# Half chunk's transposes in two PSUM tiles and earlier, outputs scaled by halves, one load behind one transpose

## The chip, the cores and the metric

The kernel runs on one core of one Trainium2 chip. The metric is the device time of one launch in microseconds (us), lower is better. The kernel before took 320.49 us, the median of three runs (318.17, 320.49 and 322.54).

## The reference

Eight batches of 576 rows go through a retention layer (attention with a decay and no softmax) with 8 heads of 64, and its output x, 512 wide, goes through a mixer of rank 32 and a two-layer MLP:

```python
scores = scale * np.matmul(q, k.transpose(0, 1, 3, 2))
Dmat = np.where(rel >= 0, gamma[:, None, None] ** rel[None, :, :], 0.0)
ret = scores * Dmat[None, :, :, :]
attn = np.matmul(ret, v)                        # x: heads side by side
h = xt @ U @ V                                  # U: 576 x 32, V: 32 x 576
u = x + h.transpose(0, 2, 1)
ch = np.maximum(u @ w_ch1, 0.0) @ w_ch2         # 512 -> 2048 -> 512
return (u + ch).astype(np.float32)
```

Inputs and output are float32; the kernel computes in bfloat16 with float32 accumulation.

## The kernel before, in words

Two batches make a pair of 1152 rows, cut into nine chunks of 128 rows (`NI = 9`). Chunk 4 (`J`) is shared: its lower 64 partitions (`LO`) hold the last rows of the even batch, its upper 64 (`HI`) the first rows of the odd one. These are the half chunks.

**The decay** is split into a factor per key row (`vscale`, put into v) and one per query row (`qscale`, put into the output), so that a running 64 by 64 state per head carries all earlier rows. A chunk needs: casts of q and k to bf16; transposes of both; scores from the transposed ones (`SC`); a causal mask (`mask`); keys times values into the state (`ST`); state copies to bf16 (`Sblk`); masked scores times values (`RV`) and queries times state (`QS`), both into one PSUM tile `po`; and the scaling of `po` by `qscale` into x (`XS`).

**Pair 0** is done in a written order. Its rows outside chunk 4 are four units of 256 rows, 0 to 3, two chunks each; functions that end in `_u` treat a unit, those in `_J` a half chunk. TensorE transposes q and k there (`T_u` at L656, `T_J` at L805). `startup` runs units 0 and 1 and `LO` (batch 0) up to u transposed (`uT`); short runs of matmuls on the identity (`warm`, L213) fill places in between. `first_stretch` goes on with the first MLP layer of batch 0 (`Y1`, L550), and between its blocks `HI` and units 2 and 3 (batch 1). In `T_J` the eight transposes, keys first, go to one PSUM tile `pst`; ScalarE copies the keys out (L757), VectorE the queries in two copies (L759). The two read one PSUM bank, and VectorE's copies wait for ScalarE's. The unit tile `po` has two banks, one for each 128 rows; `XS_u` (L737) scales both in one instruction.

Towards the end of `startup`, in order on TensorE: state products of unit 1's lower half (`ST_u`, L748), one `warm`, values of unit 1 (`RV_u`, L720), `T_J(LO)` (L811), the upper half's state products, scores of `LO` (`SC_J`, L830), `QS_u` of unit 1 (L729), transposes of x (`to_xT`, L979), `RV_J` and `QS_J` (L856, L866), the mixer's U product (`MA`, L454), the V product (L1000), and `Y1`. On VectorE: the copies of the queries, the mask of `LO` (L844), `XS_u(1)`, `XS_J(LO)` (L873).

**The later stretches**, b = 1 to 7, are lists: the MLP of batch b (in stretch 1 also the second layer of batch 0) is the main list, in a fixed order on TensorE. `merge` puts other items in where the finished share of the main list's cost reaches their place, a number from 0 to 1: `fills` (sections S, casts C, masks M, value swaps W of the next batch's chunks, and the mixer), and `places`, for each stretch the loads and the preps. `load` (L254) issues three or six DMAs on SP's queue; `prep` casts q on ScalarE (L270), k on VectorE or GpSimd (L268), scales v on GpSimd (L279) and issues a transposing DMA (`xbar`, L287) on SP. SP issues in program order: a step whose input is late holds all behind it. The mixer's `MT` also transposes u by DMA from SP (L508).

In stretch 1 the chunks of batches 2 and 3 (pair 1) are handled. Its preps are those of chunks 2 to 8 of pair 1, its loads those of chunks 4 to 8 of pair 1 and chunk 0 of pair 2:

```python
1: ((0.11, 0.24, 0.41, 0.53, 0.70, 0.85),
    (0.06, 0.20, 0.32, 0.47, 0.60, 0.73, 0.90)),
```

So the load of chunk 8 (0.70) is on SP ahead of chunk 7's transposing DMA (0.73). The section at 0.92 scores chunks 6 and 7.

The first-layer weights are one SBUF tile `w1_sb`, filled by four DMAs of 512 columns on GpSimd's queue (L219).

Of the kernel before, what the change touches and what calls it, by code (L numbers as in the profile page):

```python
# [36 lines left out]
def kernel(  # L37
# [17 lines left out]
    P = 128  # L55
# [63 lines left out]
    w1_sb = consts.tile([P, NCC, dff], BF16, name="w1_sb")  # L119
# [96 lines left out]
    W1B = 512  # L216

    def load_w1(fb):
        nc.gpsimd.dma_start(  # L219
            out=w1_sb[:, :, fb * W1B:(fb + 1) * W1B],  # L220
            in_=moe_w_ch1[:, fb * W1B:(fb + 1) * W1B].rearrange("(c p) f -> p c f", p=P),
        )
# [312 lines left out]
    def y1_items(par, by_seg=False):  # L535
# [6 lines left out]
        def Y1(f, seg):  # L542
# [6 lines left out]
            for cc in range(NCC):  # L549
                nc.tensor.matmul(  # L550
                    ps[:, 0:n, :], w1_sb[:, cc, f * P:(f + 1) * P],
                    st["uT", par][:, c0:c0 + n, cc, :],
                    start=(cc == 0), stop=(cc == NCC - 1),
                )
# [67 lines left out]
    def load_u(u, which):  # L622
        b = u // 2
        t0 = 2 * P * (u % 2) + HALF * b
        for j in which:
            dram = (q, k, v)[j]
            for hh in range(2):
                t = stage.tile([P, H, D], FP32, tag="stage", name="stage_t")
                un[u]["f", j, hh] = t
                nc.sync.dma_start(  # L630
                    out=t.rearrange("p (h j) d -> p h (j d)", j=2),
                    in_=dram[b, 4 * hh:4 * hh + 4, t0:t0 + 2 * P, :].rearrange(
                        "h (p j) d -> p h (j d)", j=2),
                )

# [23 lines left out]
    def T_u(u, j, eng):  # L659
        pst = ps_big.tile([P, 2 * NHP, P], BF16, tag="big", name="pst")  # L660
        for jj in range(2):
            for hp in range(NHP):
                nc.tensor.transpose(
                    pst[:, jj * NHP + hp, :], un[u][j][:, jj, hp * P:(hp + 1) * P], ident)
        t = qkT_pool.tile([P, 2 * NHP, P], BF16, tag="qkT", name="qkT")
# [7 lines left out]
        if eng is nc.scalar:  # L673
            nc.scalar.activation(out=o, in_=i_, func=AF.Copy)
        else:
            eng.tensor_copy(out=o, in_=i_)
# [214 lines left out]
    def pss_tile():  # L891
        return ps_s.tile([P, NHP, P], FP32, tag="pss", name="pss")

    def cast_unit(u):
        for j in (1, 0):
            for hh in range(2):
                cast_u(u, j, hh, nc.gpsimd)

    def startup():
        load_u(0, (1, 0))  # L900
        load_v_rows()
        load_u(1, (1, 0))
        load_u(0, (2,))
        load_u(1, (2,))
        load_J(LO, (1, 0, 2))
        load_u_rows()
        load_J(HI, (1, 0, 2))
        load_u(2, (1, 0, 2))
        load_u(3, (1, 0, 2))
        nc.gpsimd.memset(x_of(0, J)[HI, :], 0.0)  # L910

        warm(10)
        cast_unit(0)
        T_u(0, 1, nc.vector)
        late_consts()
        warm(5)
        nc.scalar.activation(out=V_b, in_=V_f, func=AF.Copy)
        T_u(0, 0, nc.scalar)
# [4 lines left out]
        cast_unit(1)  # L923
        T_u(1, 1, nc.scalar)
# [3 lines left out]
        T_u(1, 0, nc.scalar)  # L928
        scale_u(0, 0, nc.gpsimd)
        load_w1(0)  # L930
        scale_u(1, 0, nc.gpsimd)
        scale_u(1, 1, nc.gpsimd)
        cast_J(LO, nc.gpsimd, (0,))
        scale_J(LO, nc.gpsimd)
        load_w1(1)
        cast_J(HI, nc.gpsimd, (1, 0))
        scale_J(HI, nc.gpsimd)
        load_w1(2)
        scale_u(0, 1, nc.vector)
# [5 lines left out]

        accA = pss_tile()
        accB = ps_big.tile([P, NHP, P], FP32, tag="big", name="pss2")
        ST_u(0, LO, accA, True)
        Sblk(accA, 0)
        ST_u(0, ALL, accB, True)  # L950
        Sblk(accB, 1)
        cast_J(LO, nc.scalar, (1,))
# [19 lines left out]
        XS_u(1)  # L972
        make_ue()

        xT = [ps_big.tile([P, dm], FP32, tag="big", name="xT") for _ in range(3)]

        def to_xT(i, ccs):
            for cc in ccs:
                nc.tensor.matmul(  # L979
                    xT[cc][:, i * P:(i + 1) * P],  # L980
                    x_of(0, i)[:, cc * P:(cc + 1) * P], ident,
                    start=(i == 0), stop=True, skip_group_check=True,
                )

        for i in range(2):
            to_xT(i, range(3))
# [3 lines left out]
        MA_, _, _, _ = mixer_items(0, 0, split=True)  # L990
        MA_(steps=(0, J))
        xT.append(ps_o.tile([P, dm], FP32, tag="po", name="xT"))
        to_xT(2, range(3))
        MA_(steps=(J, J + 1))
        to_xT(3, range(3))
        for i in range(J):
            to_xT(i, (3,))
        for cc in range(NCC):
            g = slice(cc * R, (cc + 1) * R)
            nc.tensor.matmul(  # L1000
                xT[cc], st["a", 0][g, :], V4[g, HALF:HALF + 4 * P],
                start=False, stop=True, skip_group_check=True,
            )
        warm(1)
        for cc in range(NCC):
            o = st["uT", 0][:, :, cc, :]
            i_ = xT[cc].rearrange("p (s t) -> p s t", t=P)
            if cc % 2 == 0:
                nc.scalar.activation(out=o, in_=i_, func=AF.Copy)  # L1009
            else:  # L1010
                nc.vector.tensor_copy(out=o, in_=i_)

    def gated_w2(f, block):

        nc.gpsimd.tensor_copy(
            out=gate[0:1, 0:1], in_=st["y1", 1][0:1, block, P:P + 1])
        load_w2(f)

    def first_stretch():

        ys = iter([fn for _, fn in y1_items(0)])

        def y(n):
            for _ in range(n):
                fn = next(ys, None)
                if fn is not None:
                    fn()

        _, MH0, _, outs0 = mixer_items(0, 0, split=True)
        MA1, MH1, MT1, outs1 = mixer_items(0, 1, split=True)  # L1030
        y(1)
        make_uo()
        y(3)
        T_J(HI, (nc.scalar, nc.vector), ps_s, "pss")
        y(1)
        SC_J(HI)
        mask_J(HI)
        acc = pss_tile()
        ST_J(HI, acc, 0)
        Sblk(acc, 0, hps=slice(0, 2))  # L1040
        y(1)
        RV_J(HI)
        XS_J(HI)
        ST_J(HI, acc, 1)
        Sblk(acc, 0, hps=slice(2, 4))

        def unit(u, slots, last):
            for hh in range(2):
                cast_u(u, 1, hh, nc.gpsimd)
            cast_u(u, 0, 0, nc.gpsimd)  # L1050
            cast_u(u, 0, 1, nc.gpsimd)
            if last:
                load(*order[NI], (1, 0, 2), gate=True)
                load(*order[NI + 1], (1, 0, 2))
            scale_u(u, 0, nc.gpsimd)
            if not last:
                load_w1(u + 1)
            scale_u(u, 1, nc.gpsimd)
            if not last:
                y(1)  # L1060
            T_u(u, 1, nc.vector)
            T_u(u, 0, nc.scalar)
            y(2)
            SC_u(u, 0, ps_sc, "psc")
            mask_u(u, 0)
            y(1)
            ST_u(u, LO, acc, False)
            Sblk(acc, slots[1], (nc.scalar, nc.scalar) if last else (nc.vector, nc.scalar))
            SC_u(u, 1, ps_sc, "psc")
            mask_u(u, 1)  # L1070
            if not last:
                RV_u(u, 0)
                ST_u(u, HI, acc, False)
                Sblk(acc, slots[2])
            else:
                y(1)
                load(*order[NI + 2], (1, 0, 2))
                RV_u(u, 0)
            QS_u(u, 0, slots[0])
            QS_u(u, 1, slots[1])  # L1080
            RV_u(u, 1)
            XS_u(u)

        unit(2, (0, 1, 2), False)
        unit(3, (2, 3), True)
# [3 lines left out]
        xT = [None] * NCC  # L1089

# [150 lines left out]
```

## Time and profile before

| | |
|---|---|
| median of three runs | 320.49 us |
| the profiled execution's own time | 318.2 us |
| its span, first to last instruction | 316.4 us |
| TensorE (PE) busy | 306.7 us, 97% |
| VectorE (DVE) busy | 168.0 us, 53% |
| ScalarE (ACT) busy | 138.3 us, 44% |
| GpSimd (POOL) busy | 90.5 us, 29% |
| granted TensorE clock | 1.000 |

Times in the profile are from the span's start. PE is matmuls, PEld their weight loads, SPq the queue of SyncE. A row of the timeline reads: start, length, engine, line, operation, output and inputs, shapes, count, and in brackets how long the engine had been idle before and who ended that. Matmul ends are modelled, so a short wait can lie inside a row of PE. The chain of work that ended last lists start, length and instruction of each step, each released by the one above. A line can be that of a helper: L757 and L759 are `copy`, which several steps use.

### The profile page before, as it was taken

How to read it: one execution, taken by the hardware profiler on the slowest of the kernel's cores; microseconds unless marked ns; L12 is line 12 of the kernel's file. 1: busy time of each engine (PE TensorE's matmuls, PEld its weight loads, DVE VectorE, ACT ScalarE, POOL GpSimd, SP SyncE). 2: the span in 40 equal slices, each digit the busy share in tenths (PEclk: the TensorE clock that was granted, in tenths of full speed). 3: DMA queues.
4: the chain of work that ended last, by engine and by line, in shares of the span. 5: the costliest groups of instructions: out<-in, count | busy, mean ns of one | idle time of the engine just before them, and what ended most of it. 6: DMA issues, size and time to landing. Idle time of an engine off the chain costs nothing.

```text
span 316.4 us, 9192 instructions
## 1 busy us (share of the span) xinstructions
PE 306.7 (97%) x3940; PEld 168.9 (53%) x3966; DVE 168.0 (53%) x331; ACT 138.3 (44%) x285; POOL 90.5 (29%) x139
## 2 busy tenths in 40 slices
PE   8989999999999999999999999999999999999995
PEld 3564654654544454467654445467645444467544
DVE  6872656436997853993258724892368614100012
ACT  3756657760231575147820474147720463057300
POOL 6862834512322422253301430352301100200000
PEclk9999999999999999999999999999999999999999
DMA  7999999999999999999929696999634105110022
GB/s 214 274 200 285 206 206 217 199 186 244 202 204 256 250 217 155 256 238 224 185 70 209 191 214 137 216 238 233 152 64 138 68 2 85 66 67 2 0 98 70
DMA packets 149881, 53.31 MB, mean 168 GB/s; under 512 B 129008, under 2 KB 147312, under 8 KB 149840
## 3 DMA queue, kind: packets, MB, share of 16 engines
q1 hardware_dynamic: 143072, 40.40, 62.7%
q0 software_dynamic: 6768, 12.32, 16.2%
q8 instruction: 31, 0.51, 0.7%
q14 instruction: 10, 0.08, 0.1%
HBM read 36.85 MB, written 9.44 MB: 146 GB/s over the span
## 4 chain that ended last, share of the span: by engine, by line
PE 81%; DVE 7%; DMA 4%; SPq 3%; issue 2%; ACT 2%; POOL 1%; DVEq 0%; ACTq 0%; POOLq 0%
PE ps_y L550 39%; PE ps_y L584 29%; DMA qkT<-qk 2%; SPq L254 2%; DMA stage_t<-in_q_dram 2%; DVE ret L348 1%; DVE o_sb L573 1%; PE ps_y L595 1%; PE po L398 1%; DVE s_f L370 1%; PE psc L318 1%; PE ph L490 1%; DVE xt L737 1%; PE pa L454 1%; PE po L409 1%
## 5 line engine op out<-in xcount | busy, mean ns | idle before, releaser
L550 PE MATMUL ps_y<-uT,w_sb 128*128 128x512 bf16 (+3 forms) x768 | 130.3, 326 | 0.5 <-ACT uT L1009 0.4
L584 PE MATMUL ps_y<-w_sb,y 128*128 128x512 bf16 x534 | 122.6, 379 | 2.8 <-issue 1.9
L555 ACT ACTIVATE y<-ps_y 128x384 bf16<-128x384 f32 (+2 forms) x192 | 89.3, 490 | 49.8 <-PE ps_y L550 48.9
L550 PEld LDWEIGHTS <-w_sb 128*128 128x128 bf16 x768 | 71.1, 98 | 51.7 <-issue 2.1
L584 PEld LDWEIGHTS <-y 128*128 128x128 bf16 x560 | 52.7, 98 | 61.2
L573 DVE TENSOR_TENSOR o_sb<-ps_y,u 128x512 f32<-128x512 f32 (+2 forms) x38 | 25.1, 661 | 55.6 <-PE ps_y L584 53.3
L377 ACT ACTIVATE s_sb<-s_f 128x1024 bf16<-128x1024 f32 (+1 forms) x16 | 14.8, 922 | 82.1 <-DVE s_f L370 75.6
L576 POOL DMA_DIRECT2D out_dram<-o_sb x31 | 17.4, 562 | 112.7 <-DVE o_sb L573 103.1
L417 DVE TENSOR_TENSOR xt<-po,qscale 128x512 bf16<-128x512 f32 x27 | 17.6, 686 | 43.8 <-PE po L409 43.8
L279 POOL TENSOR_TENSOR vt<-stage_t,vscale 128x512 bf16<-128x512 f32 x27 | 28.1, 1042 | 41.0 <-DMA stage_t<-in_v_dram 39.0
L348 DVE TENSOR_TENSOR ret<-psc,tri 64x512 bf16<-64x512 f32 (+1 forms) x64 | 38.6, 603 | 1.2
L496 DVE TENSOR_TENSOR u<-ph,xt 128x512 bf16<-128x512 f32 (+4 forms) x33 | 22.5, 734 | 13.1 <-PE ph L490 13.0
L270 ACT ACTIVATE qk<-stage_t 128x512 bf16<-128x512 f32 x27 | 16.8, 623 | 12.0 <-DMA stage_t<-in_q_dram 11.9
L268 POOL CAST qk<-stage_t 128x512 bf16<-128x512 f32 x20 | 12.3, 617 | 18.7 <-DMA stage_t<-in_k_dram 12.7
L370 DVE TENSOR_TENSOR s_f<-inc,s_f 128x256 f32<-128x256 f32 x38 | 16.1, 423 | 2.1 <-PE inc L335 0.5
L361 DVE COPY vs<-vt 64x256 bf16<-64x256 bf16 x54 | 14.7, 271 | 1.0
L699 DVE TENSOR_TENSOR ret<-psc,triU 128x1024 bf16<-128x1024 f32 x8 | 9.6, 1220 | 5.2 <-PE psc L691 5.2
L648 POOL CAST qk<-stage_t 128x512 bf16<-128x512 f32 x16 | 9.7, 616 | 8.5 <-DMA stage_t<-in_q_dram 5.5
L213 PE MATMUL pw<-ident 128*128 128x512 bf16 x31 | 10.3, 462 | 1.4 <-POOL ident masks.py:199 1.4
L398 PEld LDWEIGHTS <-qkT 64*64 64x64 bf16 x384 | 4.7, 108 | 6.4 <-issue 5.9
L318 PE MATMUL psc<-qkT 64*64 64x64 bf16 x432 | 7.3, 196 | 0.4 <-DMA qkT<-qk 0.4
L652 POOL TENSOR_TENSOR qk<-stage_t,vscaleU 128x512 bf16<-128x512 f32 x7 | 7.3, 1059 | 1.0 <-DMA stage_t<-in_v_dram 1.0
(122 smaller groups left out, 179.1 us busy)
## 6 DMA issues: line engine op xcount, KB each, us to landing
stage_t<-in_k_dram SPq DMA_DIRECT2D x32, 256.0 KB, 4.2
stage_t<-in_q_dram SPq DMA_DIRECT2D x32, 256.0 KB, 4.7
stage_t<-in_v_dram SPq DMA_DIRECT2D x32, 256.0 KB, 5.4
out_dram<-o_sb POOLq DMA_DIRECT2D x31, 256.0 KB, 3.8
w_sb<-in_moe_w_ch_dram POOLq DMA_DIRECT2D x4, 512.0 KB, 7.6
w_sb<-in_moe_w_ch_dram POOLq DMA_DIRECT2D x8, 256.0 KB, 5.8
out_dram<-o_sb SPq DMA_DIRECT2D x4, 256.0 KB, 2.0
stage_t<-in_k_dram SPq DMA_DIRECT2D x6, 128.0 KB, 4.8
```

The lines of the kernel that those rows point to most:

```text
L270: nc.scalar.activation(out=t[rows, 0, :], in_=c["f", 0][rows].rearrange("p h d -> p (h d)"), func=AF.Copy)
L279: (eng or nc.gpsimd).tensor_tensor(out=c["v"][rows], in0=c["f", 2][rows], in1=vscale[rows, i, :, None].to_broadcast([n, H, D]), op=ALU.mult,)
L348: nc.vector.tensor_tensor(out=ret[o, n, 0:m], in0=psc[t, hl, 0:m * D].rearrange("p (b i) -> p b i", i=D), in1=tri[t, None, t].to_broadcast ...
L370: nc.vector.tensor_tensor(out=s_f[:, s, :], in0=src, in1=s_f[:, st["f_end"], :], op=ALU.add)
L377: nc.scalar.activation(out=s_sb[:, 0:n, :], in_=s_f[:, 0:n, :], func=AF.Copy)
L417: nc.vector.tensor_tensor(out=x_of(pr, i).rearrange("p (hp hl d) -> p hl hp d", hl=2, d=D), in0=po[:, :, a * SW:(a + 1) * SW].rearrange("p ...
L496: nc.vector.tensor_tensor(out=st["u", par][:, i0 - base:i0 - base + n, w].rearrange("p s (c d) -> p c s d", c=len(ccs)), in0=t[:, :, 0:n, ...
L550: nc.tensor.matmul(ps[:, 0:n, :], w1_sb[:, cc, f * P:(f + 1) * P], st["uT", par][:, c0:c0 + n, cc, :], start=(cc == 0), stop=(cc == NCC - 1),)
L555: nc.scalar.activation(out=st["y1", par][:, f, c0 * P:(c0 + n) * P], in_=ps[:, 0:n, :].rearrange("p s t -> p (s t)"), func=AF.Relu)
L573: nc.vector.tensor_tensor(out=o_sb[:, 0:n], in0=ps[:, 0:n], in1=st["u", par][:, c, w], op=ALU.add)
L576: (nc.sync if last else nc.gpsimd).dma_start(out=out_flat[r0:r0 + P, w], in_=o_sb[:, 0:n])
L584: nc.tensor.matmul(ps, st["y1", par][:, f, c * P:(c + 1) * P], w2_sb[:, f, :], start=(f == 0), stop=(f == NF - 1),)
```

## The change

`startup`, `first_stretch` and their helpers become one flat function `front`. Engine by engine, its instructions are the same in the same order, but for these:

1. `T_J` takes a PSUM tile for the keys and one for the queries. For `LO` both come from `ps_big`, for `HI` one from `ps_s` and one from `ps_o`.
2. `T_J(LO)` stands ahead of `RV_u(1, ...)` on TensorE, in the place of one `warm`; `QS_u(1, ...)` stands ahead of the upper half's `ST_u` and of `SC_J(LO)`.
3. `XS_u(1)` and `XS_u(3)` are two instructions each, 128 rows apiece; the mask of `LO` is between unit 1's two. Of unit 3, chunk 7's transposes are now written ahead of chunk 8's for two columns of x.
4. In stretch 1 the loads at 0.70 and 0.85 go to 0.76 and 0.88, the prep at 0.90 to 0.93. On SP this swaps one pair: chunk 7's transposing DMA comes ahead of chunk 8's three loads. No other order changes, on any engine.
5. `w1_sb` is four tiles of 512 columns; loads, matmuls and waits on it are the same.

```diff
-    w1_sb = consts.tile([P, NCC, dff], BF16, name="w1_sb")
+    w1_t = [consts.tile([P, NCC, W1B], BF16, name=f"w1_{n}") for n in range(dff // W1B)]
...
-    def T_J(r, engs, pool_=None, tag="big"):
+    def T_J(r, engs, k_at=None, q_at=None):
         c = ch[0, J]
-        pst = (pool_ or ps_big).tile([P, 2 * NHP, P], BF16, tag=tag, name="pst")
-        for j in (1, 0):
+        pst = {}
+        for j, (pool_, tag) in ((1, k_at or (ps_big, "big")), (0, q_at or (ps_big, "big"))):
+            pst[j] = pool_.tile([P, NHP, P], BF16, tag=tag, name="pst")
             for x in range(2):
                 for t in range(2):
                     nc.tensor.transpose(
-                        pst[:, j * NHP + 2 * x + t, r], c["qk"][r, j, (2 * t + x) * P:(2 * t + x + 1) * P],
+                        pst[j][:, 2 * x + t, r], c["qk"][r, j, (2 * t + x) * P:(2 * t + x + 1) * P],
                         ident[r, r])
...
-        copy(engs[0], c["kT"][:, :, r], pst[:, NHP:, r])
+        copy(engs[0], c["kT"][:, :, r], pst[1][:, :, r])
         o = c["qkT"][:, 0:NHP, r].rearrange("p (g x) (n t) -> p x t g n", g=2, t=2)
-        i_ = pst[:, 0:NHP, r].rearrange("p (x t) (g n) -> p x t g n", t=2, g=2)
+        i_ = pst[0][:, :, r].rearrange("p (x t) (g n) -> p x t g n", t=2, g=2)
         for x in range(2):
             copy(engs[1], o[:, x], i_[:, x])
...
         warm(1, ps_big, "big")
-        ST_u(1, LO, accB, False)
-        Sblk(accB, 2)
-        warm(1, ps_big, "big")
+        ST_u(1, LO, acc[1], False)
+        Sblk(acc[1], 2)
+        T_J(LO, (ACT, DVE))
         RV_u(1, 0)
         RV_u(1, 1)
-        T_J(LO, (nc.scalar, nc.vector))
-        ST_u(1, HI, accB, False)
-        Sblk(accB, 3)
-        SC_J(LO)
-        mask_J(LO)
         QS_u(1, 0, 1)
         QS_u(1, 1, 2)
-        XS_u(1)
+        ST_u(1, HI, acc[1], False)
+        Sblk(acc[1], 3)
+        SC_J(LO)
+        XS_u(1, 0, 1)
+        mask_J(LO)
+        XS_u(1, 1, 2)
         make_ue()
...
-        T_J(HI, (nc.scalar, nc.vector), ps_s, "pss")
+        T_J(HI, (ACT, DVE), (ps_s, "pss"), (ps_o, "po"))
...
-            XS_u(u)
+        XS_u(3, 0, 1)
+        XS_u(3, 1, 2)
...
-            1: ((0.11, 0.24, 0.41, 0.53, 0.70, 0.85),
-                (0.06, 0.20, 0.32, 0.47, 0.60, 0.73, 0.90)),
+            1: ((0.11, 0.24, 0.41, 0.53, 0.76, 0.88),
+                (0.06, 0.20, 0.32, 0.47, 0.60, 0.73, 0.93)),
```

More of the change, by code (lines that the diff above doesn't have):

```diff
@@ L672, in T_u @@
             i_ = pst.rearrange("p (j hp) t -> p j hp t", j=2)
[L673 to L676, printed above, removed]
+        copy(eng, o, i_)
     def qT(u):
@@ new lines, in mix_xT, with uT_cp, gated_w2 @@
+    def mix_xT(par):
+        for cc in range(NCC):
+            g = slice(cc * R, (cc + 1) * R)
+            nc.tensor.matmul(
+                xT[par, cc], st["a", par][g, :],
+                V4[g, (1 + par) * HALF:(1 + par) * HALF + 4 * P],
+                start=False, stop=True, skip_group_check=True,
+            )
+    def uT_cp(par, cc, eng):
+        copy(eng, st["uT", par][:, par:4 + par, cc, :],
+             xT[par, cc].rearrange("p (s t) -> p s t", t=P))
+    def gated_w2(f, block):
+        nc.gpsimd.tensor_copy(
+            out=gate[0:1, 0:1], in_=st["y1", 1][0:1, block, P:P + 1])
+        load_w2(f)
@@ L922, in startup @@
         mask_u(0, 0)
-        cast_unit(1)
-        T_u(1, 1, nc.scalar)
+        cast_u(1, 1, 0, POOL)
+        cast_u(1, 1, 1, POOL)
+        cast_u(1, 0, 0, POOL)
+        cast_u(1, 0, 1, POOL)
+        T_pe(1, 1)
+        T_cp(1, 1, ACT)
         SC_u(0, 1, ps_o, "po")
@@ L944, in startup @@
         mask_u(1, 1)
[L946 to L952, printed above, removed]
+        new_acc(0, ps_s, "pss")
+        new_acc(1, ps_big, "big")
+        ST_u(0, LO, acc[0], True)
+        Sblk(acc[0], 0)
+        ST_u(0, ALL, acc[1], True)
+        Sblk(acc[1], 1)
+        cast_J(LO, ACT, (1,))
         po_u(0, ps_sc, "psc")
@@ L989, in startup @@
         XS_J(LO)
[L990 to L1003, printed above, removed]
@@ L1004, in startup @@
-        warm(1)
[L1005 to L1031, printed above, removed]
-        make_uo()
-        y(3)
-        T_J(HI, (nc.scalar, nc.vector), ps_s, "pss")
-        y(1)
+        MA0(steps=(0, J))
@@ L1036, in first_stretch @@
+        to_xT(0, (0, 1, 2), (2,))
+        MA0(steps=(J, J + 1))
+        to_xT(0, (0, 1, 2), (3,))
+        to_xT(0, (3,), range(J))
+        mix_xT(0)
+        warm(1)
+        uT_cp(0, 0, ACT)
+        uT_cp(0, 1, DVE)
+        uT_cp(0, 2, ACT)
+        uT_cp(0, 3, DVE)
+        ys[0]()
+        make_uo()
+        ys[1]()
+        ys[2]()
+        ys[3]()
+        T_J(HI, (ACT, DVE), (ps_s, "pss"), (ps_o, "po"))
+        ys[4]()
         SC_J(HI)
         mask_J(HI)
-        acc = pss_tile()
@@ L1039, in first_stretch @@
-        ST_J(HI, acc, 0)
-        Sblk(acc, 0, hps=slice(0, 2))
-        y(1)
+        new_acc(2, ps_s, "pss")
+        ST_J(HI, acc[2], 0)
+        Sblk(acc[2], 0, hps=slice(0, 2))
+        ys[5]()
         RV_J(HI)
         XS_J(HI)
[L1044 to L1081, printed above, removed]
-            XS_u(u)
@@ L1084, in first_stretch @@
-        unit(2, (0, 1, 2), False)
-        unit(3, (2, 3), True)
+        ST_J(HI, acc[2], 1)
+        Sblk(acc[2], 0, hps=slice(2, 4))
+        cast_u(2, 1, 0, POOL)
+        cast_u(2, 1, 1, POOL)
+        cast_u(2, 0, 0, POOL)
+        cast_u(2, 0, 1, POOL)
+        scale_u(2, 0, POOL)
+        load_w1(3)
+        scale_u(2, 1, POOL)
+        ys[6]()
+        T_pe(2, 1)
+        T_cp(2, 1, DVE)
+        T_pe(2, 0)
+        T_cp(2, 0, ACT)
+        ys[7]()
+        ys[8]()
+        SC_u(2, 0, ps_sc, "psc")
@@ new lines, in front @@
+        mask_u(2, 0)
+        ys[9]()
+        ST_u(2, LO, acc[2], False)
+        Sblk(acc[2], 1, (DVE, ACT))
+        SC_u(2, 1, ps_sc, "psc")
+        mask_u(2, 1)
+        RV_u(2, 0)
+        ST_u(2, HI, acc[2], False)
+        Sblk(acc[2], 2)
+        QS_u(2, 0, 0)
+        QS_u(2, 1, 1)
+        RV_u(2, 1)
+        XS_u(2)
+        cast_u(3, 1, 0, POOL)
+        cast_u(3, 1, 1, POOL)
+        cast_u(3, 0, 0, POOL)
+        cast_u(3, 0, 1, POOL)
+        load(*order[NI], (1, 0, 2), gate=True)
@@ new lines, in front @@
+        load(*order[NI + 1], (1, 0, 2))
+        scale_u(3, 0, POOL)
+        scale_u(3, 1, POOL)
+        T_pe(3, 1)
+        T_cp(3, 1, DVE)
+        T_pe(3, 0)
+        T_cp(3, 0, ACT)
+        ys[10]()
+        ys[11]()
+        SC_u(3, 0, ps_sc, "psc")
+        mask_u(3, 0)
+        ys[12]()
+        ST_u(3, LO, acc[2], False)
+        Sblk(acc[2], 3)
+        SC_u(3, 1, ps_sc, "psc")
+        mask_u(3, 1)
+        ys[13]()
+        load(*order[NI + 2], (1, 0, 2))
+        RV_u(3, 0)
+        QS_u(3, 0, 2)
@@ L1086, in first_stretch @@
+        QS_u(3, 1, 3)
+        RV_u(3, 1)
+        XS_u(3, 0, 1)
+        XS_u(3, 1, 2)
         load_w2(0)
```

216 lines of the change are left out of this document (122 added, 94 removed).

## The prediction

> **What bounds the kernel now.** I read the busy table first, then the slices, then who waits for whom on TensorE, then the two places that the change touches. Of the page:
>
> ```profile
> span 316.4 us, 9192 instructions
> ...
> PE 306.7 (97%) x3940; PEld 168.9 (53%) x3966; DVE 168.0 (53%) x331; ACT 138.3 (44%) x285; POOL 90.5 (29%) x139
> ...
> DMA  7999999999999999999929696999634105110022
> ```
>
> TensorE is busy 306.7 of 316.4 us, so all waits together are below 10 us. The DMA engines are at 90% or more in nearly all of the first 20 slices, up to 158 us: there loads are a second bound, close beside. TensorE's waits (us in total, times, longest):
>
> ```profile
> PE psc L830 <- ACT s_sb L757: 0.4, 1, 0.4
> PE psc L318 <- DMA qkT<-qk: 0.4, 1, 0.4
> PE ps_y L550 <- ACT uT L1009: 0.4, 1, 0.4
> ```
>
> The first and third are in the stretch of batch 0 that the change reorders, the second is at the load that it moves. These and the waits hidden in PE's rows between are all there is to win.
>
> **The prologue, 16 to 24 us.** VectorE's timeline there:
>
> ```profile
> 18.32 0.50 DVE L759 COPY qkT<-pst 128x128 bf16<-128x128 bf16 x2 [0.83 <-ACT s_f L757]
> 19.16 0.68 DVE L844 TENSOR_TENSOR ret<-psc,triJ 64x512 bf16<-64x512 f32 x1 [0.34 <-PE psc L830]
> 19.77 1.21 DVE L737 TENSOR_TENSOR xt<-po,qscale 128x1024 bf16<-128x1024 f32 x1
> 20.90 0.67 DVE L873 TENSOR_TENSOR xt<-poJ,qscale 64x512 bf16<-64x512 f32 x1
> ```
>
> The queries' copies wait for ScalarE's copy of the keys (17.90 to 18.29), the scores of LO wait for them (18.67), the mask for the scores, `XS_u(1)` for the mask, and `XS_J` for `XS_u(1)`, though its own products end at 20.70. Then the chain goes U product, V product, uT copies, first MLP block at 23.36.
>
> After the change, from the rows of before: TensorE ends the lower `ST_u` at 16.74; 8 transposes 0.34 (17.08), `RV_u` 0.57 (17.65), `QS_u` 0.55 (18.20; its second state copy is ready at 17.56), upper `ST_u` 0.37 (18.57), scores 0.46 (19.03). The casts that `T_J` reads end at 15.64 (GpSimd) and 16.59 (ScalarE), in time. ScalarE's key copy stays behind the state copies, 17.56 to 17.95; VectorE copies the queries when `XS_u(0)` ends, 17.49 to 18.0. So the scores now wait for nothing and end only 0.1 sooner: four steps of TensorE have moved in front of them. What moves most is `XS_u(1)`: first half 18.02 to 18.7, mask 19.06 to 19.74, second half to 20.36. `RV_J` and `QS_J` follow the mask and end at 20.59 (0.1 sooner), so `XS_J` starts at 20.63, not 20.90: the first MLP block comes **0.27 us** sooner. The removed filler costs nothing: transposes stand in its place. The extra instruction costs about 0.07 (two of 128x512 take 1.28 to 1.29 back to back, one of 128x1024 1.21 to 1.23); it is in the sum, and hidden: `XS_J` waits for TensorE.
>
> Does 0.27 us reach the end? At 31.4 us TensorE transposes unit 2, whose second query half GpSimd casts late, because its load is late:
>
> ```profile
> 31.22 0.62 POOL L648 CAST qk<-stage_t 128x512 bf16<-128x512 f32 x1 [2.33 <-DMA stage_t<-in_q_dram]
> ```
>
> The cast ends at 31.84; the transposes (16 from 31.38) reach that half with the 11th, at about 31.93. Slack: 0.09 us. At 35.41 the state products start while GpSimd still scales the second half of v (to 35.51); they reach it at about 35.63, slack 0.1. Those loads were issued on SP at 20 to 25 us behind other loads, with no wait for TensorE between, so they don't come sooner. I count **0.1 us** gained (ends: 0, as the slack is read off modelled matmul ends, and 0.27).
>
> **Chunk HI and unit 3.** The scores of HI start at 28.42, when the MLP block before them ends (28.43): the copies were not what they waited for. 0, at best 0.05. `XS_u(3)` runs 45.48 to 46.71 and chunk 7's and 8's transposes start at 46.76, after an MLP block that ends at 46.63. By halves chunk 7 is ready at 46.16, chunk 8 at 46.8: two transposes (0.1) go early, the others up to 0.1 later. 0, ends -0.15 and +0.1.
>
> **The swap on SP, 92 to 106 us.** The chain of work in order of time:
>
> ```profile
> 90.36 2.21 SPq L287
> 92.56 0.05 issue
> 92.62 1.32 SPq L254
> ...
> 94.04 0.52 SPq L254
> ...
> 94.60 1.63 SPq L254
> ...
> 96.39 6.58 DMA qkT<-qk
> 102.98 0.04 issue
> 103.02 0.32 PE psc L318 x16
> ```
>
> SP issues chunk 6's transpose, then chunk 8's three loads, then chunk 7's transpose, which lands 6.58 us later while TensorE waits 0.44 us (102.57 to 103.02). In ScalarE's timeline chunk 7's last cast is ready before SP comes to it:
>
> ```profile
> 94.43 0.61 ACT L270 ACTIVATE qk<-stage_t 128x512 bf16<-128x512 f32 x1
> ```
>
> It ends at 95.04, and it is behind a state cast on ScalarE, which is not moved. So the transpose goes out at 95.1, 1.3 us sooner. Landing takes 2.7 (shortest), 4.8 (median) to 8.4 us (longest) over the 27 of this line: 97.8 to 103.5. I take at most 6.58, the transpose's own row, now with three loads fewer ahead: 101.7 or sooner, ahead of 102.5. The wait goes: **0.44 us**. At 8.4 it would be 1.0 instead, a loss of 0.56.
>
> The Trainium skill bears on that choice: "DMA: Bandwidth & Descriptors", section "Queues, rings and completion order", says that each DMA engine takes one queue's descriptors in ring order. By that rule the transpose no longer stands behind the three loads and lands nearer to 2.7 than to 6.58; the sum is the same, the loss of 0.56 excluded. No row of before shows this transpose without them.
>
> What waits now: SP has nothing to issue from 92.56 to 95.1, and behind the waiting transpose stand chunk 8's loads, the transposing DMA of u (L508), chunk 0's loads and chunk 8's transpose. Chunk 7's transpose takes SP 1.2 to 3.7 us, median 1.98 (before: 3.70, with full rings); loads then from 97.1, 2.6 to 3.6 us. u's transpose goes out at 99.8 to 100.8 against 100.20, lands 4.3 later (its row), 105.1 at the latest; the MLP block that reads it starts at 106.13, less the gain 105.6. Nothing is lost. Chunk 8's casts: GpSimd comes to its k at 102.75, behind an output's issue; k from 97.1 lands by 101.7 (4.6, its row). Its transpose, at 105.24 before, is wanted at 113.69, landed by 111.1: 2.5 us of slack. During SP's pause the DMA engines have work: v of chunk 7 lands at 94.4, chunk 6's transpose at 96.8.
>
> The places 0.85 to 0.88 and 0.90 to 0.93 change no engine's order: 0. So does `w1` in four tiles: same DMAs, same waits; bounds plus or minus 0.1 from the 0.82 to 0.94 us that an issue of it takes on GpSimd.
>
> **The sum**, on the profiled execution: 0.1 + 0 + 0.44 = 0.54 us less, span 315.9, own time 318.2 - 0.5 = 317.7. That execution is 2.3 below the median of the runs shown; on the median, 320.49 - 0.5 = **320.0 us**. Three runs lie 4.4 us apart, so this kernel's measurement can tell about 2% (6.4 us) from no change, and not this.
>
> **Rivals.**
> - *The prologue's gain passes whole* (0.27, and 0.1 at unit 3): needs unit 2's query load to land sooner; against it, 2.33 us of idle GpSimd before that cast. For it: a slack read off modelled ends. 0.8 less: 319.7. Chance 0.2.
> - *The change does not do what it says*: DMA engines over 90% busy deliver chunk 7's transpose no sooner for an earlier issue, and the prologue's gain is eaten at 31.9. 320.5. Chance 0.15.
> - *Slower: SP's pause is passed on.* If SP does not catch up the 2.5 us (92.56 to 95.1), u's transpose goes out at 102.7, lands at 107.0 and TensorE stands 1.4 us before the first MLP block of batch 2. It decides from an issue later than 101.3 (105.6 - 4.3). For it: SP issues without a pause from 85 to 140 us, its issues stretched to 3.7 us by full rings. Against it: emptier rings are faster ones, down to 1.2. 1.4 - 0.54 = 0.9 more: 321.4. Chance 0.15.
> - *The clock falls.* The first ten fillers took 4.45 us, 0.445 each, later ones 0.27: TensorE was slow at the start. Losing a filler could bring that back over the 5 us of work to 23 us, by 0.445/0.27: 3 us more, 323. Rows speak against it: granted clock 1.0, longest gap 0.44. Chance 0.02. The Trainium skill, "TensorE: Matmul & The Clock Gate", section "Part 1: The HAM clock gate", has the clock fall after an idle window of about 3.4 us; no run here shows one; by that rule the chance is none.
>
> The forecast has 0.48. **The range**: the cases lie from 319.7 to 321.4, and single runs 2.3 below to 2.05 above their median; 317.2 to 322.9 takes both in. All cases lie within 2%; for what I have not seen I leave 0.03 for faster and 0.05 for slower by over 2%, and 0.92 within.
>
> **What would show it.** The VectorE copies (L759) released by TensorE at about 17.5, not by ScalarE; `XS_u(1)` in two rows around the mask; the first MLP block at 23.1. Unit 2's transposes or state products waiting 0.1 to 0.2 us for GpSimd. Chunk 7's transposing DMA out at about 95 and no wait of the scores for it; u's transpose out by 101. Wrong it would be if TensorE waits for u's transpose or a chunk's at 106, 122 or 135 us, or if unit 2's casts come sooner.

## The result, and the profile after

The changed kernel takes **321.94 us** (median; 318.7 to 328.1), beside 318.17 us (317.16 to 322.95) for the kernel before in the same comparison. The ratio is **1.0091, interval 1.0064 to 1.0117**: some 2.9 us slower, where 0.5 us faster was forecast. The medians take in every execution; the ratio is of means and leaves out those more than 1.5% above the fastest of their kernel, here two of the changed one (326.67 and 328.1 us) and three of the other. 321.94 lies in the forecast range, and the change is within 2%, but its sign was wrong.

The profiled execution of the changed kernel has a span of 317.9 us (own time 319.64), 1.5 more than before. Line numbers of the changed kernel are smaller by one in the chunks' code (L549, L317, L507, L253, L286 for L550, L318, L508, L254, L287). Head of its page:

```profile
span 317.9 us, 9217 instructions
...
PE 308.8 (97%) x3965; PEld 168.1 (53%) x3965; DVE 169.1 (53%) x333; ACT 137.9 (43%) x285; POOL 90.8 (29%) x139
```

TensorE's two longest waits (total in us, times, longest):

```profile
PE ps_y L549 <- DMA uT<-u: 1.8, 1, 1.8
PE pw L214 <- POOL ident masks.py:199: 1.4, 1, 1.4
```

The scores no longer wait for chunk 7's transpose (0.4 before). In its place the first MLP block of batch 2 stands 1.8 us for the transposing DMA of u, the longest wait of the profile. (The second, 1.4 us for the identity, is at the kernel's start, and the kernel before has it too.)

**The prologue** did more than foreseen. VectorE's timeline:

```profile
17.30 0.49 DVE L745 COPY qkT<-pst 128x128 bf16<-128x128 bf16 x2
18.04 0.69 DVE L723 TENSOR_TENSOR xt<-po,qscale 128x512 bf16<-128x512 f32 x1 [0.24 <-PE po L715]
18.66 0.68 DVE L831 TENSOR_TENSOR ret<-psc,triJ 64x512 bf16<-64x512 f32 x1
19.27 0.67 DVE L723 TENSOR_TENSOR xt<-po,qscale 128x512 bf16<-128x512 f32 x1
20.37 0.68 DVE L860 TENSOR_TENSOR xt<-poJ,qscale 64x512 bf16<-64x512 f32 x1 [0.43 <-PE poJ L853]
```

The copies of the queries wait for nobody, `XS_u(1)` is two rows around the mask, and `XS_J` starts at 20.37 (before: 20.90). TensorE's first MLP block starts at 22.84, before at 23.36: **0.52 us** sooner, and the first `po` products of batch 2's stretch at 75.51 instead of 75.96: 0.45 of it is still there.

Most of that is lost further on, at a place that the prediction doesn't name. VectorE adds to the state in four instructions at about 209 us, before and then after:

```profile
208.06 1.86 DVE L370 TENSOR_TENSOR s_f<-inc,s_f 128x256 f32<-128x256 f32 x4
```

```profile
209.14 0.41 DVE L369 TENSOR_TENSOR s_f<-inc,s_f 128x256 f32<-128x256 f32 x1
210.02 1.34 DVE L369 TENSOR_TENSOR s_f<-inc,s_f 128x256 f32<-128x256 f32 x3 [0.46 <-DVE s_f L369]
```

After the first of the four VectorE now stands 0.46 us; ScalarE's state cast and its evictions follow later, and TensorE's MLP block there (64 matmuls) takes 9.44 us instead of 9.07: 0.36 us lost. All 13 traces with the new front have this (9.43 to 9.45), all four with the old one have not (9.07 or 9.08), whatever the places. What stops VectorE is open; none of the front's edits was tried by itself.

**The swap** is where the time goes. The chain of work in order of time (start, length, what):

```profile
95.50 3.70 PE ps_y L584 x17
99.20 7.92 DMA uT<-u
107.12 0.05 issue
107.17 7.08 PE ps_y L549 x32
```

And SP's own timeline, after and then before:

```profile
88.54 7.29 SPq L286 DMA_TRANSPOSE qkT<-qk  x2
95.89 0.57 SPq L253 DMA_DIRECT2D stage_t<-in_k_dram  x1
96.51 1.70 SPq L253 DMA_DIRECT2D stage_t<-in_q_dram  x1
98.25 0.84 SPq L253 DMA_DIRECT2D stage_t<-in_v_dram  x1
99.20 3.77 SPq L507 DMA_TRANSPOSE uT<-u  x1
```

```profile
96.39 3.70 SPq L287 DMA_TRANSPOSE qkT<-qk  x1
100.20 2.25 SPq L508 DMA_TRANSPOSE uT<-u  x1
102.50 0.59 SPq L254 DMA_DIRECT2D stage_t<-in_k_dram  x1
```

The row of 7.29 us is chunk 6's transpose, a wait, and chunk 7's transpose. Who ended SP's waits says how long it stood, and the windows say what the DMA engines did in the meantime (stretch; then five engines, granted clock, DMA share, GB/s). SP's waits between 84 and 106 us, after:

```profile
SPq L286 <- ACT qk L269: 4.7, 2, 4.1
```

Windows of after:

```profile
93.00:96.00 3.00, 3.00 (x47) 1.40 (x40) 2.85 (x7) 1.31 (x3) 1.27 (x2) 1.00 0.42 150
96.00:99.00 3.00, 3.00 (x16) 1.37 (x14) 2.96 (x6) 0.00 (x0) 0.14 (x1) 1.00 1.27 121
```

Windows of before:

```profile
93.00:96.00 3.00, 2.90 (x46) 1.33 (x46) 2.92 (x7) 1.31 (x3) 1.48 (x2) 1.00 0.68 146
96.00:99.00 3.00, 2.94 (x14) 1.36 (x14) 2.97 (x5) 0.63 (x1) 0.10 (x1) 1.00 1.22 314
```

SP stands 4.1 us in front of chunk 7's transpose until ScalarE has cast chunk 7's q (93.85 to 94.46, behind a state cast). The DMA engines run low: 121 GB/s from 96 to 99 us, where before they moved 314. Their busy share does not fall in these three (1.27 against 1.22) but in the three before (0.42 against 0.68), and from 94 to 95 us they move nothing at all. Then SP issues chunk 8's three loads and, right behind them, u's transpose. That goes out at 99.20, *sooner* than before (100.20), but lands **7.92 us** later, where it took 4.3 before: at 107.12, not 104.5. The sum at the start of the block that reads it: 106.13 before, less 0.45 (prologue), less 0.44 (chunk 7's wait), plus 1.84 (new wait) is 107.08; the row says 107.17. So the block is 1.04 us late, and with the 0.36 at 210 us that is 1.40 of the 1.5 us between the two spans.

### The profile page after: what moved, and what is told of

The parts are those of the page before. It is cut to its first block, busy times and chain, and to the rows that moved or that the text cites. A ratio compares the mean times of both kernels' runs of the same rounds, so it can differ in the third digit from the quotient of the medians.

```text
span 317.9 us, 9217 instructions
## 1 busy us (share of the span) xinstructions
PE 308.8 (97%) x3965; PEld 168.1 (53%) x3965; DVE 169.1 (53%) x333; ACT 137.9 (43%) x285; POOL 90.8 (29%) x139
## 3 DMA queue, kind: packets, MB, share of 16 engines
HBM read 36.85 MB, written 9.44 MB: 146 GB/s over the span
## 4 chain that ended last, share of the span: by engine, by line
PE 79%; DMA 11%; DVE 3%; SPq 3%; issue 1%; POOL 1%; ACT 1%; POOLq 0%; DVEq 0%; ACTq 0%
PE ps_y L549 36%; PE ps_y L584 35%; DMA stage_t<-in_v_dram 5%; DMA w<-in_moe_w_ch_dram 3%; DMA uT<-u 2%; SPq L926 2%; DMA stage_t<-in_k_dram 2%; PE po L397 1%; PE psc L317 1%; PE ph L489 1%; PE ps_y L595 1%; PE po L408 1%; PE pa L453 1%; PE inc L334 1%; DVE ret L347 1%
## 5 line engine op out<-in xcount | busy, mean ns | idle before, releaser
L549 PE MATMUL ps_y<-uT,w 128*128 128x512 bf16 (+3 forms) x768 | 130.6, 326 | 2.5 <-DMA uT<-u 1.8
L584 PE MATMUL ps_y<-w_sb,y 128*128 128x512 bf16 x560 | 126.2, 379 | 0.0
L549 PEld LDWEIGHTS <-w 128*128 128x128 bf16 x768 | 71.0, 98 | 54.4 <-issue 2.4
L743 ACT ACTIVATE qkT<-pst 128x1024 bf16<-128x1024 bf16 x5 | 6.3, 1258 | 2.4 <-PE pst L649 2.4
```

The costliest lines, as they stand in the source:

```text
L549: nc.tensor.matmul(ps[:, 0:n, :], w1_t[f * P // W1B][:, cc, f * P % W1B:f * P % W1B + P], st["uT", par][:, c0:c0 + n, cc, :], start=(cc == ...
L584: nc.tensor.matmul(ps, st["y1", par][:, f, c * P:(c + 1) * P], w2_sb[:, f, :], start=(f == 0), stop=(f == NF - 1),)
```

## The experiments

The two theories after the result. *Order*: u's transpose is late because three loads stand directly ahead of it on SP's queue. *Pause*: it is late because SP's standing let the DMA engines run dry and the backlog then passes at once. A rival to both: the front's edits cost something later. The comparisons with a ratio ran beside the kernel before on the same chip.

**The prologue alone** (the changed kernel with the old places) and **the swap alone** (the kernel before with the new places):

```diff
-            1: ((0.11, 0.24, 0.41, 0.53, 0.76, 0.88),
-                (0.06, 0.20, 0.32, 0.47, 0.60, 0.73, 0.93)),
+            1: ((0.11, 0.24, 0.41, 0.53, 0.70, 0.85),
+                (0.06, 0.20, 0.32, 0.47, 0.60, 0.73, 0.90)),
```

> The changed kernel with the old places in stretch 1: all of the prologue's edits and the four weight tiles, without the swap on SP. Theory S (the loss is the swap: SP stands 4.1 us before chunk 7's transpose, the DMA engines run dry, and u's transpose then goes out right behind chunk 8's loads and lands late): no wait for u's transpose; first MLP block of batch 0 at about 22.9 us as in the changed kernel; 0 to 0.5 us faster than before, as the wait for chunk 7's transpose may take the gain back. Rival F (the loss is in the front: filler gone, new order, weight tiles, a clock that dips in some runs): about 2.9 us slower than before, as the changed kernel.

> The kernel before with the new places only: the one swap on SP, nothing else. Theory S: 1 to 3 us slower than before, with a wait of 1.4 to 1.8 us of the first MLP block of batch 2 for u's transpose at about 107 us. Rival F: no slower than before, up to 0.4 us faster.

The prologue alone: 317.65 us beside 318.41, ratio 0.9989 (0.9957 to 1.0021); no wait for u. The swap alone: 319.54 us, ratio 1.0025 (0.9995 to 1.0055). TensorE's waits with the swap alone:

```profile
PE ps_y L550 <- DMA w_sb<-in_moe_w_ch_dram: 1.8, 1, 1.8
PE ps_y L550 <- DMA uT<-u: 1.4, 1, 1.4
```

So the wait for u belongs to the swap: it is there without the new front, and gone with the new front and the old places. (The wait for `w_sb`, a block of first-layer weights in the front, is in a front that the swap does not touch; more below.) By their times neither part is told from no change: both intervals hold 1. And the two do not add up to the whole: -0.8 and +1.1 us by the medians (-0.4 and +0.8 by the ratios) against +3.8 (+2.9). A TensorE that comes sooner waits longer for the same late transpose, 1.8 instead of 1.4; the clock, below, brings some of the rest, and what is left is open.

**Chunk 8's loads behind u's transpose**, the pause left as it is:

```diff
-            1: ((0.11, 0.24, 0.41, 0.53, 0.76, 0.88),
+            1: ((0.11, 0.24, 0.41, 0.53, 0.80, 0.88),
```

> The changed kernel with chunk 8's loads one step later, at 0.80: on SP they come behind u's transpose too. Theory S with the order as its main part (three loads ahead of u's transpose in the rings): u's transpose lands 4 to 5 us after its issue, no wait for it, 0.4 to 0.9 us faster than before. Theory S with the dry DMA engines as its main part: the wait for u goes, but chunk 8's or a later transpose is late by 1 to 2 us in its place, and the time stays above before. Rival F: 2.9 us slower, as the changed kernel.

318.69 us, ratio 1.0012 (0.9982 to 1.0042); 3.2 below the changed kernel's median. SP's timeline and its waits between 84 and 110 us:

```profile
88.14 7.29 SPq L286 DMA_TRANSPOSE qkT<-qk  x2
97.56 1.33 SPq L507 DMA_TRANSPOSE uT<-u  x1
98.94 0.77 SPq L253 DMA_DIRECT2D stage_t<-in_k_dram  x1
```

```profile
SPq L286 <- ACT qk L269: 4.6, 2, 4.2
```

SP stands as long (4.2 us), and the traffic falls as low (80 GB/s from 96 to 99 us), but u's transpose lands 5.0 us after its issue and TensorE does not wait for it. The pause alone makes nothing late here: the order does. The place has a price of its own. Chunk 8's q now comes so late that its cast on ScalarE (108.90 to 109.53) stands in front of the MLP's evictions, and TensorE waits 0.8 us for one.

**A shorter pause**, the order left as it is: chunk 7's prep earlier, so that ScalarE casts its q ahead of the state cast.

```diff
-                (0.06, 0.20, 0.32, 0.47, 0.60, 0.73, 0.93)),
+                (0.06, 0.20, 0.32, 0.47, 0.60, 0.71, 0.93)),
```

> The changed kernel with chunk 7's prep at 0.71, which changes one thing: ScalarE casts chunk 7's queries ahead of the state cast, so that SP can issue its transpose when GpSimd's cast of the keys is done, at about 92.1 us instead of 94.5. Order on SP as in the changed kernel. Theory S with the dry engines as its main part: SP's pause falls from 4.1 to about 1.7 us, the wait for u from 1.8 to 0 to 0.5 us, the time to 0 to 0.9 us below before. Theory S with the order as its main part: u's transpose still lands 6 to 8 us after its issue behind three loads; as it goes out some 2 us sooner the wait falls too, but later loads stay as they are. Rival F: 2.9 us slower.

318.39 us, ratio 1.0007 (0.9971 to 1.0043). In its trace SP waits 0.7 us for the cast, u's transpose still goes out behind the three loads, at 101.74, and lands 5.7 us later, where 6 to 8 was expected of the order alone. TensorE does not wait for it, but it comes to the block that reads u only at 108.6, so this trace doesn't show what the landing would cost a TensorE on time; that the loss is gone is in the ratio. The profiled execution (span 319.2) lost its time elsewhere, the largest piece at an earlier chunk's transpose that landed 7.5 us after its issue:

```profile
PE psc L317 <- DMA qkT<-qk: 1.2, 1, 1.2
```

All traces together, by what is directly ahead of u's transpose on SP and by SP's longest wait for ScalarE's side between 84 and 106 us:

| ahead of u's transpose | SP's wait | traces | issue to landing, us |
|---|---|---|---|
| chunk 7's transpose | 0 to 2.2 | before and two more executions of it; the new front with old places, five traces | 4.3 to 5.5 |
| chunk 7's transpose, loads moved behind u | 4.2; none | load behind u; both mends | 5.0; 4.9 |
| chunk 8's loads | 0.7 to 1.9 | short pause; the last of the changed kernel's four further executions (below) | 5.7; 5.7 |
| chunk 8's loads | 3.8 to 4.4 | the changed kernel's other four traces; swap alone | 7.4 to 8.0 |

Only with the loads ahead *and* the long pause does it reach 7.4 us and more. What the pause adds rests on one trace, that of the short pause: in the last further execution SP stood 2.3 us between the loads and u's transpose, until VectorE had written u, so that the loads had that time to pass. (The column counts waits for ScalarE alone. SP also stands directly in front of u's transpose for u itself: up to 2.1 us with the old order, 4.0 with both mends.)

**Both mends together** (chunk 8's loads at 0.80, chunk 7's prep at 0.71):

> The changed kernel with chunk 8's load at 0.80 (behind u's transpose on SP) and chunk 7's casts prepared at 0.71 (ScalarE's half ahead of the state cast). If the loss is u's transpose behind the three loads, lengthened by SP's pause, this has neither: no wait for u, SP's pause before chunk 7's transpose under 2 us, 318.2 to 318.8, about as each mend alone, since each alone already took the wait away. Rival: the pause costs DMA traffic that is paid elsewhere as well, then both together are 0.3 to 0.6 better than either, 317.9 or below.

319.91 us beside 318.07, ratio 1.0056 (1.0017 to 1.0094): above either mend alone, against both expectations, though seven executions don't tell them apart: the intervals overlap. u's transpose lands 4.9 us after its issue, and nothing waits for it. The trace's longest waits behind its start are:

```profile
PE pst L649 <- POOL qk L634: 1.2, 1, 1.2
PE ps_y L549 <- ACT y L555: 1.0, 1, 1.0
```

The second, at 112.7 us, is the price of the place 0.80, as above; the first and one of 0.6 us for first-layer weights are in the front, which this kernel shares with the prologue alone. No mend beats the old order.

**The changed kernel again**, four more profiled executions, to see what single ones lose:

> The changed kernel itself once more, for a second profiled execution and paired times: its profiled execution took 319.64 us, most of its 22 runs about 322, and the swap alone costs 1.1 us of the median, the prologue alone gains 0.8. Theory S: about 321.9 again; in an execution near the median the wait for u's transpose at 107 us is longer than 1.8 us (3 to 4), and nothing else is new. Rival G: the added 2 us lie elsewhere, as a wait for the last block of first-layer weights at 41 us (1 to 2 us, seen in two other profiles) or as a clock that dips for a window.

> The same, for a third profiled execution. Theory S: a wait for u's transpose of 1.8 to 4 us, by which its time follows. Rival G: the wait for u stays near 1.8 us and the time follows a wait for weights or the clock.

> The changed kernel for another profiled execution: over a third of its runs show a granted clock of 0.994 or 0.995 and take about 322 to 324 us, against one in forty of the kernel before. If this execution is such a one, rival G expects a stretch of about 3.4 us at half the clock, and the question is where: theory S expects it at the wait for u's transpose (105 to 112 us), rival F in the front (0 to 50 us). If it is none: a wait for u of 1.8 to 2 us and about 319.5 to 320.8 us.

> The same as the execution before it: with the clock at 0.995 about 322 to 324 us and a stretch at half the clock, at 105 to 112 us by theory S, at 0 to 50 us by rival F; without it 319.5 to 320.8 us.

Medians and single times: 321.82 (four executions; ratio 1.0132, 1.0056 to 1.0208), 320.78, 321.17 and 321.03 us. Three of the four traces have the wait for u (1.8, 2.0, 2.1 us); the 3 to 4 us that theory S gave for an execution near the median did not come, and the second has 1.3 us of waits for GpSimd's casts in the front besides. The first and the third of the four make a pair: in both the block that reads u starts at the same time, 107.12 and 107.13, but the `po` products behind it at 114.14 and 115.83. The window behind the wait in the third:

```profile
107.00:111.00 4.00, 3.87 (x11) 1.43 (x12) 1.92 (x5) 0.86 (x2) 1.13 (x2) 0.57 1.08 232
```

and in the first:

```profile
107.00:111.00 4.00, 3.88 (x18) 1.76 (x19) 2.22 (x5) 2.41 (x5) 1.51 (x2) 1.00 0.94 235
```

In the third the granted clock is 0.57 on the mean from 107 to 111 us, and 11 matmuls are recorded where the first has 18. In half-microsecond windows it is 0.50 from 107.5 to 110.5, some 3.4 us with its edges; half of 3.4 is 1.7, and 1.69 us is the difference. **After a wait of 2 us the clock can fall to half for 3.4 us, and that costs 1.7 us on top of the wait.** The fourth execution has it at another place: its scores wait 1.47 us for an earlier chunk's transpose at 91 us, and the clock is 0.50 from 93.2 to 96.6.

It does so in a part of the executions. One such stretch in 318 us makes a mean granted clock of 0.995. Of the 29 executions of the changed kernel whose clock is on record 13 have 0.995 or less, of the kernel before, beside which the experiments ran, 1 of 79. In the first comparison the changed kernel's executions at 0.994 or 0.995 have a median of 322.5 us (7), those at a full clock 320.6 (13). But the lowered clock does not belong to the wait for u alone. With the old places the new front has it in 8 of 38 executions, with the mends in 5 of 31, and the swap alone, which has the wait, in 1 of 12. Four traces show the fall: one behind the wait for u, one behind the chunk's transpose, and two in the front (both below).

The kept traces say when it falls. The clock's changes in them lie whole multiples of 3.41 us behind its first rise (30, 26, 3 and 10 of them at the four falls), and each fall lasts one such window. In the third execution 2.07 us of idle TensorE lie in the one window ahead of the fall. In the second the wait of 2.0 us is split by two windows, 0.78 and 1.35 us, and the clock stays. The length alone does not decide: 1.84 and 1.76 us in one window (the first profile of the changed kernel, and the first of the four) left the clock at 1.0, while 1.48 to 1.78 us were enough ahead of the other three falls.

**The weights of the front sooner.** The prologue alone showed a wait of 1.1 us at 41 us for a block of `w1`, which GpSimd issues behind its scaling of v. Moved ahead of that:

```diff
-        scale_u(2, 0, POOL)
         load_w1(3)
+        scale_u(2, 0, POOL)
         scale_u(2, 1, POOL)
```

> The prologue alone (old places) with the load of the last block of first-layer weights issued one step sooner on GpSimd, ahead of the first scaling of unit 2's values. If the gain of the prologue is eaten by the late weights at 41 us (1.1 us in the prologue's profile), that wait goes and the kernel is 0.8 to 1.5 us faster than before; rival: the sooner transfer only takes the DMA engines from unit 2's values, the scaling and the state products are late in its place, and the time is that of the prologue alone (317.65 us) or above.

319.1 us beside 319.09, ratio 1.0006 (0.997 to 1.0041): no gain, as the rival had it. The wait for the weights is gone from its trace, and three for GpSimd's casts are there, 1.9 us together. Here the clock fell too, from 40.4 to 43.8 us, after two waits of 0.74 us within two.

**The prologue alone once more, and single executions** of it and of the kernel before, to see whether the front's 0.45 us reaches the end:

> The front's edits alone with the old places, again, for a narrower interval against the kernel before: 0.998 (0.45 to 0.8 us sooner) if the 0.45 us seen at 48 us reaches the end; 1.000 or above if it is lost at the late block of w1 at 41 us, as the wait of 1.1 us in its first profile would have it.

> The front's edits alone, one look. If the slower half of its executions (319.4 to 320.7 against 317.0 to 317.9) is loads of the front that land late, an execution of 319 or more shows TensorE waiting 0.5 to 2 us between 30 and 48 us for a block of w1 or a cast of unit 2 or 3, and its unit 3 starts that much later; one of 317 to 318 shows none, as in the run before this one. Rival: the slower ones lose it after 48 us, at the chunks' loads.

> The kernel before, one look. If the new front alone brings the late loads, TensorE waits for no load or cast between 30 and 48 us, and the time is 317.2 to 318.5. Rival: the old front has them as well, at times, since the swap alone, with the old front, had 1.8 us there.

> As the first look: the wait in the front, or none, goes with the time.

> As the second look: no wait for a load or a cast in the front, or one at times.

The longer comparison gave 319.73 us beside 318.07, ratio 1.0016 (0.9982 to 1.005), with executions from 316.95 to 322.68; the ratio leaves out the two above 322. With the first one (0.9989) that is no difference that can be told. The traces, by the start of the first `po` products of batch 2's stretch:

| | `po` at, us | span, us | waits of the front over 0.5 us |
|---|---|---|---|
| before, profiled | 75.96 | 316.4 | none |
| before, two further executions | 75.79; 75.91 | 315.6; 315.8 | none; 0.6 for GpSimd, ahead of a transpose |
| prologue alone, first | 76.12 | 316.3 | 1.1 for weights |
| prologue alone, again | 75.15 | 315.3 | none |
| its two single executions | 78.85; 75.66 | 319.5; 316.0 | 1.8 for a scaling of v; 0.7 for a cast |

Without a wait the new front is 0.6 to 0.8 us sooner at that place, and that execution has the shortest span of all, though 0.36 of it goes at 210 us. But the old front has waits as well (0.6 here, 1.8 with the swap alone), and a single one of 0.7 to 1.1 eats the gain. The first single execution of the prologue alone missed both expectations: at 12.67 us one scaling of v on VectorE took 3.46 us, 0.68 in all 16 other traces; TensorE waited 1.8 us for it, and the clock was 0.50 from 17.5 to 20.9. That step is ahead of all that the change touches. What stretched it is open.

## Why the prediction was wrong

**The step that failed is in the swap: "u's transpose goes out at 99.8 to 100.8 ..., lands 4.3 later (its row), 105.1 at the latest ... Nothing is lost."** The issue was estimated well, 99.20 here. The landing was not: 7.92 us. The 4.3 came from a row in which chunk 7's transpose stood ahead, and it was used for a queue in which chunk 8's three loads stand ahead. Every trace with the loads elsewhere has 4.3 to 5.5, and moving only the loads brings it back to 5.0. The prediction took the same neighbours into account for the transpose that it wanted to see sooner ("now with three loads fewer ahead"), and not for the one behind which those loads were put.

The Trainium skill's "DMA: Bandwidth & Descriptors", section "Queues, rings and completion order", was cited there for the first half: an engine takes one queue's descriptors in ring order. By that rule u's transpose stands behind the three loads; the order experiment, 5.0 against 7.92 us, agrees. What the prediction drew from it for chunk 7's transpose, a landing nearer to 2.7 than to 6.58, did not come out: 4.8 us.

**"During SP's pause the DMA engines have work"** failed as well. The pause was 4.1 us, not 2.5: chunk 6's transpose went out at 88.54 instead of 90.36 and took less time, and the cast that ends the pause came only 0.6 sooner. The 2.5 was one execution's: in the two further executions of the kernel before, chunk 6's transpose went out at 88.82 and 88.94 as well. The traffic fell to 121 GB/s. With a pause of 0.7 us the same order landed in 5.7, in one trace; how much of the price is the pause's is not shown beyond that.

**The slower rival** ("SP's pause is passed on", 0.15, 0.9 us more) named the right wait at the right block and gave it a wrong mechanism. Its decision point, an issue of u's transpose after 101.3, was not reached in the profiled execution: the issue was 2 us ahead of it, and TensorE stood all the same. Its price of 1.4 us for the wait was measured as 1.4 with the old front, 1.8 to 2.1 with the new. Had the prediction asked for the landing instead of the issue, a landing of more than 6.4 us, from 99.20 to its 105.6, would have been the condition; the 8.4 that it quoted as the longest of its line for chunks' transposes lay in reach.

**Chunk 7's wait, 0.44 us**: right. It is gone, and chunk 7's transpose lands 4.8 us after its issue, below the 6.58 taken as the bound.

**The prologue** was right in its mechanism and undersized, 0.27 predicted and 0.52 measured at the first MLP block. The queries' copies and the scores of `LO` followed the working to 0.3 us; the scores started at 18.30, where ends of TensorE's steps laid row after row gave 18.57, because neighbouring steps overlap; the mask came at 18.66, not 19.06. The cap ("I count 0.1 us gained", from unit 2's second query cast at 31.22) did not hold: 0.45 was left at 75 us. That cast starts at 28.43 in the changed kernel's trace, and in the kernel before too it was early in the two further executions (27.92, and done by 28.52). A slack of 0.09 us had been read from one execution's late load. In the medians neither 0.1 nor 0.45 shows: 0.36 goes at 210 us, and the front's loads and casts vary by more from execution to execution.

**Chunk `HI`, unit 3, the places without a change of order and the four tiles of `w1`** were costed at nothing, and no wait in the profiled execution is put down to them. They were not tried one by one. The 0.36 us at 210 us comes with the new front and its tiles, not with the places; which of their edits brings it is open.

**The clock** had 0.02, for a filler less in the front, with "longest gap 0.44" against it (that leaves out the 1.4 us at the kernel's start). In the profiled execution the clock stayed at 1.0. It did fall at that place in one execution of the prologue alone (17.5 to 20.9 us), behind a wait of 1.8 us and not shown to be the filler's doing; and it fell behind the new wait for u, which the prediction had not put together with it: a lost wait and a lowered clock can come as one case, worth 2.1 and 1.7 us in one execution here.

**What stays open.** The profiled executions differ by 1.5 us, the comparison by 2.9. The clock brings part of that: without the two executions that the ratio leaves out, 11 of 27 have it lowered, and times 1.7 that is 0.7 us on the mean. Why the new front lowers it so often, with the swap and without, is not shown. Five executions of the first comparison took 321.7 to 322.6 us at a full clock; no trace of one of them exists. Two of the nine traces with the new places, and none of the eight with the old, have a wait of 1.2 to 1.5 us for an earlier chunk's transpose; too few to put it down to the places.

## What to carry to other kernels

When two steps on one queue change places, price both: the one that moves up gets the other's neighbours and the next one behind inherits what moved down. A time from issue to landing belongs to the row's queue, to what stands directly ahead and whether the queue has just stood still; it is not a property of the transfer, so give it the range of its line when the neighbours change. And a slack of a tenth of a microsecond, read in one execution at a load whose landing varies by microseconds, is neither a cap nor a gain.

## What the runs showed of the hardware

- The same transposing DMA of u took 4.3 to 8.0 us from issue to landing over 17 traces, by its place in the queue and by a pause ahead of it, and an issue 1.0 us sooner landed 2.6 us later.
- The granted clock fell to 0.50 for 3.4 us after TensorE had idled 1.5 to 2.1 us, or twice 0.74, in some executions and not in others with the same wait. The Trainium skill's "TensorE: Matmul & The Clock Gate", section "Part 1: The HAM clock gate", has the clock fall after at least one idle window of about 3.4 us, and the window run free. The length of the stretch at half clock agrees with that window, and so do the four falls, each a whole number of 3.41 us behind the clock's first rise; the idle time does not, since 1.48 us of a window were enough, and 1.84 in another were not.
- VectorE stood 0.46 us between two state updates at 209 us in 13 of 13 traces with the new front, and in none of four with the old. Its cause is open.
